# Second bias seeded into the down accumulators, SiLU read from PSUM, and a chunk's last down products done tile by tile

## The chip, the core and the metric

The kernel runs on one core of a Trainium2 chip. Its time is the device time of one execution in microseconds (us). It is written in a tile language: the program names its tiles and pools, buffers of a pool rotate under a tag, and each engine executes its own instructions strictly in the order in which they stand in the program. The engines are TensorE (PE in the profile; its weight loads are PEld), VectorE (DVE), ScalarE (ACT), GpSimd (POOL) and SyncE (SP), which here only issues transfers. Transfers are issued from SP and from ScalarE.

## What is computed

A gated block over x of 2048 tokens and 512 channels: an attention over a short dilated window, multiplied by the SiLU of an MLP, added to x. Everything is float32.

```python
xn = layernorm(x)                                   # over 512 channels, no affine part
# attention: 32 heads of 16, each token sees itself and 7 earlier ones, 2 apart
qkv = xn @ wqkv                                     # 512 -> 3 * 512
s = softmax(q . k[pos - 2*w] / 4, w = 0..7) . v     # positions before 0 are masked
s = s @ wo                                          # 512 -> 512
# MLP: 512 -> 1792 -> 512, squared ReLU
h = maximum(xn @ w1 + b1, 0) ** 2
g = silu(h @ w2 + b2)
out = x + s * g
```

## The kernel before

**Precision.** A product that needs float32 accuracy is done as three products of a faster 32-bit form. Each operand is split into a high part (ScalarE rounds it, `high`) and a low part (the difference, `low`, on VectorE or GpSimd), and TensorE forms high x high, high x low and low x high (`PASSES`). A tile with a leading axis of 2 holds the two parts. A product of 512 columns is the unit in which TensorE works.

**First stage, the projections.** 16 token tiles of 128 are taken in pairs (`for a in range(2, NT, 2)`). `norm` normalises a tile, `shuffle` writes it through four transfers into `xb`, `trans` transposes it on VectorE into PSUM, and `highx` and `lowx` split it into `xt`. From pair 4 on, `pair_of_seven` forms q and k of the two tiles from seven half-size products instead of eight: sums of parts of x (`Sf`, split into `S`) meet sums of weights (`T1` to `T4`), whose parts are made by `split_sum`. Three accumulators (`pm`) and one or two more (`pq`) share four PSUM buffers of the tag `acc`. `u2` keeps one part product until the last sum, which VectorE forms into `stg`. `plan` says behind which of six steps of a pair each piece of work for the next pair is issued; `n` shifts the preparation of the next pair by whole steps. q, k and v go through memory (`sq`, `sk`, `sv`), since the attention wants another layout. Normalised and transposed x of tiles 4 to 15 goes to memory too (`sx`), to be read again by the MLP.

**The attention** is a generator (`attention`). For each unit of 256 tokens VectorE does four multiplications with the keys (`pr`) and four reductions (`L`), the softmax with ScalarE and GpSimd, then four multiplications with the values (`pv`) and four reductions (`v`). `pump` is called between the products and issues as much of this VectorE work as the program's own clock of TensorE allows, so that VectorE's order is fixed when the program is built. Loads of k, q and v are issued from ScalarE; results go to memory (`so`) and come back as `oq` (`load_o`) for the output projection (`trans_o`, `lowo`, `out_product`, into `pw`).

**Second stage, the MLP**, in four chunks of 512 tokens (`for c in range(NCH)`), each of four tiles `j`. `up(c, f)` multiplies the chunk's transposed x (`xT[c]`) with 128 of the 1792 hidden columns, 12 products; ScalarE then applies bias and ReLU in place in PSUM, squares into the high part of `h`, and squares once more, into `hf` or in place; GpSimd or VectorE subtracts to get the low part. `down(pb, f, j)` adds three products for tile j into its accumulator `pb[j]`; the four of them use the four `acc` buffers. `down` follows `up` by two values of f. At a chunk's end stand the downs of f = 12 and 13, f by f. Then `gate` copies each accumulator with ScalarE to `z`, GpSimd adds the second bias `b2t`, and after the next chunk's first two ups `silu` applies SiLU in place. In the last chunk VectorE adds the bias. `finish` multiplies `z` by the output projection, adds x and stores. x of the next chunk is loaded by `load_xT` behind `up(c, 13)`, in two transfers, into the one buffer that the chunk leaves.

Of the kernel before, what the change touches and what calls it, by code (L numbers as in the profile page):

```python
# [57 lines left out]
def body(ctx: ExitStack, tc: tile.TileContext, x, wqkv, wo, w1, b1, w2, b2, out):  # L58
# [141 lines left out]
            G.memset(mask[:GR, :(W - 1 - w) * DIL, w], -1e9)  # L200

    b1t = const.tile([P, NF], F32, name="b1t")

    sq = dram.tile([GR, S, CH], F32, name="sq")
# [195 lines left out]


    NT = S // P
    mv, means, rs, shifts, xn, xb, pTs, xt, xT, seen, Sf, Sp = ({} for _ in range(12))

    def moments(t, st):
        mv[t] = px.tile([P, 2], F32, name=f"mv{t}", tag="mv", bufs=2)
# [40 lines left out]

    def place(t):  # L450
        if t < TPC:
            xt[t] = xT[0][:, t]
        else:
            xt[t] = pxT.tile([P, 2, KT, P], FR, name=f"xt{t}", tag="xt", bufs=4)

    def shuffle(t):

# [37 lines left out]
    def copy_quarter(a):  # L495

        _, pb = quarters(a)
        Sf[a] = hpool.tile([P, 4, 2 * P], F32, name=f"Sf{a}", tag="h", bufs=3)
        A.activation(Sf[a][:, 3], pb[:, 0], AF.Copy)
        seen[a, "copy"] = clock["V"] + 1600  # L500

# [12 lines left out]
    def sum_parts(a, half):  # L514
        n = 2 * half
        flat = Sf[a][:, n:n + 2].rearrange("p j m -> p (j m)")
        if (a, half) not in Sp:
            Sp[a, half] = hpool.tile([P, 2, 2, 2, P], FR, name=f"S{a}_{half}", tag="h", bufs=3)
        return (*(Sp[a, half][:, i].rearrange("p j k n -> p (j k n)") for i in range(2)), flat)

    def high_sums(a, half):
# [53 lines left out]
        done[1][t // 2] = clock["PE"]  # L575

    def load_xT(c):
        xT[c] = xTa.tile([P, TPC, 2, KT, P], FR, name=f"xU{c}", tag="xT")
        for j in range(0, TPC, 2):
            A.dma_start(xT[c][:, j:j + 2].bitcast(F32), sx[c][:, j:j + 2])  # L580

    hs = {}

    def up(c, f):
        ph = psH(f"ph{c}_{f}")
        n = 0
        for kt in range(KT):
            for a, b in PASSES:
                PE.matmul(ph.rearrange("p (j n) -> p j n", n=P), w12[f][:, a, 0, kt * P:(kt + 1) * P],
                          xT[c][:, :, b, kt, :], start=n == 0, stop=n == 11)  # L590
                n += 1
        if f == NF - 1 and c + 1 < NCH:
            load_xT(c + 1)
        h = hpool.tile([P, 2, 512], FR, name=f"h{c}_{f}", tag="h", bufs=3)
        A.activation(ph, ph, AF.Relu, bias=b1t[:, f:f + 1])
        A.activation(h[:, 0], ph, AF.Square)

        pool = c or f < 2 or f > 11
        full = hpool.tile([P, 512], F32, name=f"hf{c}_{f}", tag="hf") if pool else ph
        A.activation(full, ph, AF.Square)  # L600
        if pool:
            G.tensor_sub(h[:, 1], full, h[:, 0].bitcast(F32))
        hs[f] = h, None if pool else ph, clock["PE"] + 2000
# [16 lines left out]
    stats(0)  # L620
    high(*wq_parts(1, 0))
    norm(0)
    xT[0] = xTa.tile([P, TPC, 2, KT, P], FR, name="xT0", tag="xT")
    place(0)
    pT = [psT(f"pxT0_{kt}") for kt in (0, 2)]
    for kt in range(KT):
# [1 line left out]
    stats(1)  # L628
    low(*wq_parts(1, 0), V)

    x0 = hpool.tile([P, D], F32, name="xT0f", tag="h", bufs=3)
# [58 lines left out]
    flush(clock["PE"])  # L690

    split_sum(T1, V)
    split_sum(T4, V)
    pump(LATE)


# [59 lines left out]
    def pair_of_seven(a):  # L756

        b, last = a + 1, a + 2 == NT
        new_stg(a, 1)
        new_stg(a, 0)  # L760
        q, k = stgs[0], stgs[1]
        sums_ps, first, five = (psA(f"pm{a}_{n}") for n in range(3))
        u2 = pstg.tile([P, GR, CH], F32, name=f"u2_{a}", tag="u2")
# [12 lines left out]

        def seventh():
            product(sums_ps, part_s(a, 2), T3, False)
            A.activation(q[:, :, 1], heads(sums_ps), AF.Copy)
            G.tensor_add(k[:, :, 1], k[:, :, 1], q[:, :, 1])  # L780
            product(five, part_s(a, 3), K1, False)
            not_before(clock["PE"])
            V.tensor_add(k[:, :, 0], u2, heads(five))
            store_qkv(b, 1)
            beside(a, 3)

        if last:
            for f in range(2):
                up(0, f)
                pump()  # L790
            lowh(0)
        qkv(b, 2, seventh)
        beside(a, 4)
        product(sums_ps, part_x(b, 1), T4, False)
        A.activation(q[:, :, 1], heads(sums_ps), AF.Copy)
        store_qkv(b, 0)
        beside(a, 5)

    for a in range(2, NT, 2):
        if a >= TPC:  # L800
            for t in (a, a + 1):
                queue(sx[t // TPC][:, t % TPC], xt[t].bitcast(F32))
        (pair_of_seven if a in SEVEN else pair)(a)
        if a == NT - 4:
            dma(b1t, b1.rearrange("(f p) -> p f", p=P))
    pump()
    lowh(1)
    p1ctx.close()


    p2 = ctx.enter_context(tc.tile_pool(name="p2", bufs=1))
    pws, gs = {}, {}
# [57 lines left out]

    xrs = {}

# [10 lines left out]
        dma(tile_rows(out, t)[:, cols], z[:, cols])  # L883

    wot = p2.tile([P, 2, 4, 512], FR, name="wot")
    b2t = p2.tile([P, D], F32, name="b2t")
    rwo = {}

    for c in range(NCH):
        last = c == NCH - 1  # L890
        pb = [psA(f"pb{c}_{j}") for j in range(TPC)]
        t0 = c * TPC
        room = ROOM if c else ROOM0
        for f in range(2, NF):
# [1 line left out]
            if c == 0:  # L896
                next_w()
            pump()
            if c == 0 and f == 8:
                dma(b2t, b2[None, :].to_broadcast([P, D]))  # L900
            if c == 0 and f in (3, 6):

                i = f // 6
# [34 lines left out]
            if f == 11:  # L938
                for i in range(2):
                    lowo(t0 + i)  # L940
            if f >= 12:
                load_o(c * 2 + 1, last and f > 12)
# [67 lines left out]
```

## Time and profile before

| | |
|---|---|
| median of 3 runs | 493.02 us (491.42 to 495.7) |
| profiled execution | 491.57 us |
| its span, first to last instruction | 489.7 us |
| granted TensorE clock, mean | 0.996 |
| busy share: TensorE, VectorE, ScalarE, GpSimd | 98%, 87%, 48%, 47% |
| bytes moved | 81.47 MB |

In profile rows of groups, the form is: line, engine, operation, output from inputs by the program's names, shapes, count, busy time and mean of one, and idle time before with what ended it. Almost all work stands at line 87, the helper that records every operation in program order, so names of tiles tell more than lines. In timeline rows the first two numbers are start and length, and several like instructions are merged with their count; the pipelined products overlap, so a row's length is a little more than its count times their distance. ACTq and SPq rows are issues of transfers. Rows of windows give, per stretch, its length, busy time and count of PE, PEld, DVE, ACT and POOL, the granted clock as a share of full speed, the share of the transfer engines, and GB/s.

### The profile page before, as it was taken

The page shows a single profiled execution, that of the slowest core. Times are in us where ns is not written, and L with a number is a line of the kernel's source. Part 1 is how long each engine was busy: PE and PEld are TensorE (multiplying, and loading weights), DVE is VectorE, ACT ScalarE, POOL GpSimd, SP SyncE. Part 2 cuts the span into 40 slices and gives each one's busy share as a digit, 9 for nine tenths or more (in the row PEclk, how much of TensorE's full clock was granted, in tenths as well). Part 3 has the DMA queues.
Part 4 walks back from the last instruction along what each step waited for, and adds up shares of the span by engine and source line. Part 5 has one row for each costly group of instructions (what it writes and reads, how often), then busy time and mean ns, then how long its engine had stood idle before and what let it go on. Part 6 is the DMA issues. An engine that isn't in the chain of part 4 may idle for free.

```text
span 489.7 us, 5949 instructions
## 1 busy us (share of the span) xinstructions
PE 481.4 (98%) x2118; PEld 395.1 (81%) x2118; DVE 426.5 (87%) x356; ACT 233.0 (48%) x417; POOL 232.3 (47%) x174
## 2 busy tenths in 40 slices
PE   8999999999999999998999999999999999999997
PEld 5888688888888888886888888888888888888886
DVE  5978858987789699996999999699999999999744
ACT  5557597646545655234432333554233364423331
POOL 1325142133665678266847353765534396355310
PEclk9999999999999999998999999999999999999999
DMA  8899999899768984762526356525452763313132
GB/s 289 216 271 271 305 274 259 194 277 299 212 173 201 270 197 129 219 153 37 157 54 165 86 128 211 125 86 124 124 128 56 241 146 107 82 35 93 44 129 88
DMA packets 65530, 81.47 MB, mean 166 GB/s; under 512 B 6108, under 2 KB 49372, under 8 KB 64732
## 3 DMA queue, kind: packets, MB, share of 16 engines
q1 hardware_dynamic: 61180, 54.87, 40.0%
q10 hardware_dynamic: 4320, 26.22, 21.6%
q8 instruction: 17, 0.28, 0.2%
q14 instruction: 13, 0.11, 0.1%
HBM read 50.60 MB, written 27.32 MB: 159 GB/s over the span
## 4 chain that ended last, share of the span: by engine, by line
PE 89%; DVE 4%; issue 3%; POOL 1%; ACT 1%; DMA 1%; ACTq 0%; POOLq 0%; DVEq 0%
PE pb L87 28%; PE ph L87 28%; PE pq L87 13%; PE pm L87 11%; PE pw L87 8%; DVE v L87 1%; DVE pv L87 1%; POOL h L87 1%; POOL z L87 1%; DMA x<-in_A_x 1%; DVE L L87 0%; PE pxT L87 0%; ACT z L87 0%; ACT ph L87 0%; ACT w L87 0%
## 5 line engine op out<-in xcount | busy, mean ns | idle before, releaser
L87 PE MATMUL pb<-w,h 128*128 128x512 f32 x672 | 162.5, 392 | 1.9 <-POOL h L87 1.9
L87 PEld LDWEIGHTS pb<-w,h 128*128 128x128 f32 x672 | 127.1, 189 | 28.8 <-POOL h L87 2.3
L87 POOL TENSOR_TENSOR h<-hf,h 128x512 fp32r<-128x512 f32 x46 | 78.7, 1712 | 101.5 <-ACT hf L87 92.9
L87 PE MATMUL ph<-xU,w 128*128 128x512 f32 x504 | 120.6, 389 | 0.0
L87 PEld LDWEIGHTS ph<-xU,w 128*128 128x128 f32 x504 | 94.7, 188 | 19.7
L87 ACT ACTIVATE ph<-ph,b1t 128x512 f32<-128x512 f32 x56 | 37.0, 662 | 140.4 <-PE ph L87 128.9
L87 DVE TENSOR_TENSOR pr<-k,q 128x2048 f32<-128x2048 f32 x32 | 82.1, 2566 | 3.9 <-DMA q<-sq 3.4
L87 DVE TENSOR_TENSOR pv<-v,L 128x2048 f32<-128x2048 f32 x32 | 77.4, 2419 | 2.0 <-POOL L L87 1.2
L87 DVE TENSOR_REDUCE v<-pv 128x256 f32<-128x2048 f32 x32 | 73.0, 2281 | 0.8
L87 DVE TENSOR_REDUCE L<-pr 128x128 f32<-128x2048 f32 x32 | 73.0, 2281 | 0.7
L87 PE MATMUL pw<-wot,oT 128*128 128x512 f32 (+1 forms) x204 | 45.9, 376 | 0.0
L87 PEld LDWEIGHTS pw<-wot,oT 128*128 128x128 f32 x204 | 36.8, 188 | 7.1
L87 PE MATMUL ph<-xT,w 128*128 128x512 f32 x168 | 40.2, 389 | 0.0
L87 POOL TENSOR_TENSOR w<-w1r,w 128x512 fp32r<-128x512 f32 x14 | 22.5, 1608 | 33.0 <-ACT w L87 33.0
L87 PEld LDWEIGHTS ph<-xT,w 128*128 128x128 f32 x168 | 31.5, 188 | 6.5
L87 PE MATMUL pm<-wq,S 128*128 128x512 f32 x144 | 36.2, 392 | 0.2 <-ACT S L87 0.2
L87 PE MATMUL pq<-wq,xt 128*128 128x512 f32 x144 | 35.8, 390 | 0.0
L87 ACT ACTIVATE h<-ph 128x512 fp32r<-128x512 f32 x56 | 33.5, 599 | 1.8
L87 ACT ACTIVATE hf<-ph 128x512 f32<-128x512 f32 x46 | 27.4, 595 | 11.4 <-POOL h L87 11.4
L87 PEld LDWEIGHTS pm<-wq,S 128*128 128x128 f32 x144 | 26.7, 188 | 7.1 <-ACT S L87 0.7
L87 PEld LDWEIGHTS pq<-wq,xt 128*128 128x128 f32 x144 | 26.9, 188 | 6.2 <-ACT stg L87 0.6
L87 PE MATMUL pq<-wq,xT 128*128 128x512 f32 x132 | 30.9, 393 | 0.0
(83 smaller groups left out, 507.6 us busy)
## 6 DMA issues: line engine op xcount, KB each, us to landing
k<-sk ACTq DMA_DIRECT2D x8, 960.0 KB, 7.4
v<-sv ACTq DMA_DIRECT2D x8, 960.0 KB, 8.4
sx<-xt SPq DMA_DIRECT2D x12, 512.0 KB, 5.5
xU<-sx ACTq DMA_DIRECT2D x6, 1024.0 KB, 7.4
x<-in_A_x SPq DMA_DIRECT2D x16, 256.0 KB, 4.9
sk<-stg SPq DMA_DIRECT2D x8, 512.0 KB, 4.0
sq<-stg SPq DMA_DIRECT2D x8, 512.0 KB, 6.5
sv<-stg SPq DMA_DIRECT2D x8, 512.0 KB, 4.9
```

Of the source, the lines that this page charges most:

```text
L87: return tc.keep_in_program_order(f(*a, **k))
```

## The change

The second bias is loaded early, beside `b1t`, and kept. Before a chunk's downs ScalarE copies it into each accumulator (`begin`), and all downs add to it (`start=False`). At a chunk's end the downs of f = 10 are held back behind `up(c, 13)`; the downs of f = 12 and 13 are done tile by tile, and behind each tile ScalarE applies SiLU from PSUM to `z` (`gate`) and seeds the accumulator for the next chunk. The separate bias additions and `silu` are gone.

The transposed x keeps the channel block `kt` as its outer axis: `sx` is written in pieces of 1 KB instead of 4 KB, and `load_xT` loads a chunk in four transfers, one for each `kt`. In the projections, pair 4 prepares the next pair one step earlier (`n` is 1 instead of 2 there); two of the weight differences and the split of T4 move from VectorE to GpSimd and into pair 2; `Sf`, `S` and `h` have four buffers instead of three; `u2` moves into the buffers of `hf` and `x`. `load_o` of a chunk's second unit is issued at other places.

```diff
-    sx = {c: dram.tile([P, TPC, 2, KT, P], F32, name=f"sx{c}") for c in range(1, NCH)}
+    sx = {c: dram.tile([P, KT, TPC, 2, P], F32, name=f"sx{c}") for c in range(1, NCH)}
...
     def load_xT(c):
-        xT[c] = xTa.tile([P, TPC, 2, KT, P], FR, name=f"xU{c}", tag="xT")
-        for j in range(0, TPC, 2):
-            A.dma_start(xT[c][:, j:j + 2].bitcast(F32), sx[c][:, j:j + 2])
+        xT[c] = xTa.tile([P, KT, TPC, 2, P], FR, name=f"xU{c}", tag="xT")
+        for kt in range(KT):
+            A.dma_start(xT[c][:, kt].bitcast(F32), sx[c][:, kt])
...
-        h = hpool.tile([P, 2, 512], FR, name=f"h{c}_{f}", tag="h", bufs=3)
+        h = hpool.tile([P, 2, 512], FR, name=f"h{c}_{f}", tag="h", bufs=4)
...
-            V.tensor_sub(*(raws[s, kt + i] for s, kt in (d, x0, x1)))
+            (G if d == (0, 2) else V).tensor_sub(*(raws[s, kt + i] for s, kt in (d, x0, x1)))
...
     split_sum(T1, V)
-    split_sum(T4, V)
     pump(LATE)
...
-        n, t = (2 if a < 6 else 0), a + 2
+        n, t = {2: 2, 4: 1}.get(a, 0), a + 2
...
-    for i, w in enumerate((T2, T3)):
+    for i, w in enumerate((T2, T3, T4)):
         at(2, 1 + i, split_sum, w, G)
...
-                queue(sx[t // TPC][:, t % TPC], xt[t].bitcast(F32))
+                queue(sx[t // TPC][:, :, t % TPC], xts[t].bitcast(F32))
...
+    def begin(c, j):
+
+        pbs[c, j] = psA(f"pb{c}_{j}")
+        A.activation(pbs[c, j], b2t, AF.Copy)
+
     def down(pb, f, j):
         h, w = hs[f][0], w12[f]
         for n, (a, b) in enumerate(PASSES):
             PE.matmul(pb[j], h[:, a, j * P:(j + 1) * P], w[:, b, 1, :],
-                      start=f == 0 and n == 0, stop=f == NF - 1 and n == 2)
+                      start=False, stop=f == NF - 1 and n == 2, skip_group_check=True)
...
     def gate(c, j, pb):
         z = gs[c, j] = piece(f"z{c}_{j}")
-        if c == NCH - 1:
-            V.tensor_add(z, pb[j], b2t)
-            silu(c, j)
-        else:
-            A.activation(z, pb[j], AF.Copy)
-            G.tensor_add(z, z, b2t)
-
-    def silu(c, j):
-        A.activation(gs[c, j], gs[c, j], AF.Silu)
+        A.activation(z, pb[j], AF.Silu)
...
-            if not (last and f == NF - 1):
+            downs = [f - 2]
+            if last and f == NF - 1:
+                downs = []
+            elif not last and f > NF - 3:
+                downs = [f - 3, f - 2] if f == NF - 1 else []
+            for i in downs:
                 for j in range(TPC):
-                    down(pb, f - 2, j)
+                    down(pb, i, j)
...
         if not last:
-            for i in range(2):
-                for j in range(TPC):
+            for j in range(TPC):
+                for i in range(2):
                     down(pb, NF - 2 + i, j)
-                if i == 0:
-                    pump(room)
-            pump()
-            for j in range(TPC):
+                pump(room if j < 2 else -SLACK)
                 gate(c, j, pb)
+                begin(c + 1, j)
             for i in range(2):
                 up(c + 1, i)
                 pump(ROOM)
                 lowh(i)
-            for j in range(TPC):
-                silu(c, j)
+                load_o(c * 2 + 1, False)
             out_product(t0 + 1, psT(f"pw{t0 + 1}"))
             pump(ROOM)
```

More of the change, by code (lines that the diff above doesn't have):

```diff
@@ L202, in body @@
     b1t = const.tile([P, NF], F32, name="b1t")
+    b2t = const.tile([P, D], F32, name="b2t")
     sq = dram.tile([GR, S, CH], F32, name="sq")
@@ L404, in body @@
     NT = S // P
-    mv, means, rs, shifts, xn, xb, pTs, xt, xT, seen, Sf, Sp = ({} for _ in range(12))
+    mv, means, rs, shifts, xn, xb, pTs, xt, xT, seen, Sf, Sp, xts = ({} for _ in range(13))
     def moments(t, st):
@@ L451, in place @@
         if t < TPC:
-            xt[t] = xT[0][:, t]
+            parts = xT[0][:, :, t]
         else:
-            xt[t] = pxT.tile([P, 2, KT, P], FR, name=f"xt{t}", tag="xt", bufs=4)
+            parts = xts[t] = pxT.tile([P, KT, 2, P], FR, name=f"xt{t}", tag="xt", bufs=4)
+        xt[t] = parts.rearrange("p k a n -> p a k n")
     def shuffle(t):
@@ L497, in copy_quarter @@
         _, pb = quarters(a)
-        Sf[a] = hpool.tile([P, 4, 2 * P], F32, name=f"Sf{a}", tag="h", bufs=3)
+        Sf[a] = hpool.tile([P, 4, 2 * P], F32, name=f"Sf{a}", tag="h", bufs=4)
         A.activation(Sf[a][:, 3], pb[:, 0], AF.Copy)
@@ L517, in sum_parts @@
         if (a, half) not in Sp:
-            Sp[a, half] = hpool.tile([P, 2, 2, 2, P], FR, name=f"S{a}_{half}", tag="h", bufs=3)
+            Sp[a, half] = hpool.tile([P, 2, 2, 2, P], FR, name=f"S{a}_{half}", tag="h", bufs=4)
         return (*(Sp[a, half][:, i].rearrange("p j k n -> p (j k n)") for i in range(2)), flat)
@@ L622, in body @@
     norm(0)
-    xT[0] = xTa.tile([P, TPC, 2, KT, P], FR, name="xT0", tag="xT")
+    xT[0] = xTa.tile([P, KT, TPC, 2, P], FR, name="xT0", tag="xT")
     place(0)
@@ L629, in body @@
     low(*wq_parts(1, 0), V)
-    x0 = hpool.tile([P, D], F32, name="xT0f", tag="h", bufs=3)
+    x0 = hpool.tile([P, D], F32, name="xT0f", tag="h", bufs=4)
     for kt in (0, 2):
@@ L762, in pair_of_seven @@
         sums_ps, first, five = (psA(f"pm{a}_{n}") for n in range(3))
-        u2 = pstg.tile([P, GR, CH], F32, name=f"u2_{a}", tag="u2")
+        home = dict(pool=px, tag="x", bufs=4) if last else dict(pool=hpool, tag="hf")
+        u2 = home.pop("pool").tile([P, GR, CH], F32, name=f"u2_{a}", **home)
         product(sums_ps, part_x(a, 0), Q0)
@@ L805, in body @@
             dma(b1t, b1.rearrange("(f p) -> p f", p=P))
+            dma(b2t, b2[None, :].to_broadcast([P, D]))
     pump()
@@ L885, in body @@
     wot = p2.tile([P, 2, 4, 512], FR, name="wot")
-    b2t = p2.tile([P, D], F32, name="b2t")
     rwo = {}
@@ L890, in body @@
         last = c == NCH - 1
-        pb = [psA(f"pb{c}_{j}") for j in range(TPC)]
+        if c == 0:
+            for j in range(TPC):
+                begin(c, j)
+        pb = [pbs[c, j] for j in range(TPC)]
         t0 = c * TPC
@@ L940, in body @@
                     lowo(t0 + i)
-            if f >= 12:
-                load_o(c * 2 + 1, last and f > 12)
-            if not (last and f == NF - 1):
+            if f == 11 or (last and f > 11):
+                load_o(c * 2 + 1, f > 12)
+            downs = [f - 2]
[4 more added lines that the diff above has]
+            for i in downs:
                 for j in range(TPC):
-                    down(pb, f - 2, j)
+                    down(pb, i, j)
             pump(room)
@@ L952, in body @@
         if not last:
-            for i in range(2):
-                for j in range(TPC):
+            for j in range(TPC):
+                for i in range(2):
                     down(pb, NF - 2 + i, j)
-                if i == 0:
-                    pump(room)
-            pump()
-            for j in range(TPC):
+                pump(room if j < 2 else -SLACK)
                 gate(c, j, pb)
+                begin(c + 1, j)
             for i in range(2):
```

6 lines of the change are left out of this document (2 added, 4 removed).

## The prediction

> **What bounds the kernel now.** I read the page's busy table first, then the chain of waits that ended last, and then the TensorE timeline wherever that chain leaves TensorE.
>
> ```profile
> span 489.7 us, 5949 instructions
> PE 481.4 (98%) x2118; PEld 395.1 (81%) x2118; DVE 426.5 (87%) x356; ACT 233.0 (48%) x417; POOL 232.3 (47%) x174
> ...
> 303.66 5.44 PE ph L87 x24
> ```
>
> TensorE is busy for 98% of the span, and the chain shows its pace: 24 products of 512 columns in 5.44 us, 0.2267 us each. The change neither adds nor removes a product, so it can win only where products start later than this pace allows. I walked the TensorE timeline of the whole span and compared each group's start with the previous start plus count times 0.2267. Behind the opening 11 us, two places miss by more than 0.15 us. The first is in the projections:
>
> ```profile
> 55.38 1.98 PE L87 MATMUL pm<-wq,xt 128*128 128x512 f32 x8
> 57.82 1.20 PE L87 MATMUL pm<-wq,xt 128*128 128x512 f32 x4 [0.47 <-DVE xt L87]
> 59.27 1.92 PE L87 MATMUL pm<-wq,S 128*128 128x512 f32 x6 [0.25 <-ACT S L87]
> 61.21 3.02 PE L87 MATMUL pq<-wq,xt 128*128 128x512 f32 x12
> ```
>
> From 55.38, 8 + 4 + 6 products should take 4.08 us and end at 59.46; the next group starts at 61.21. That is 1.75 us lost, for xt, for S, and for a free accumulator. The second place is the start of MLP chunk 1:
>
> ```profile
> 223.55 0.61 PE L87 MATMUL pb<-w,h 128*128 128x512 f32 x2
> 226.04 4.14 PE L87 MATMUL pb<-w,h 128*128 128x512 f32 x10 [1.87 <-POOL h L87]
> 230.02 2.24 PE L87 MATMUL ph<-xU,w 128*128 128x512 f32 x9
> ...
> 224.00:226.00 2.00, 0.17 (x1) 0.00 (x0) 0.86 (x1) 0.00 (x0) 1.98 (x1) 1.00 0.00 0
> 226.00:228.00 2.00, 1.96 (x6) 1.52 (x7) 0.00 (x0) 1.95 (x3) 1.27 (x1) 0.63 0.04 8
> 228.00:229.00 1.00, 1.00 (x4) 0.81 (x3) 0.41 (x1) 1.00 (x3) 0.00 (x0) 0.50 0.00 0
> 229.00:230.00 1.00, 1.00 (x4) 0.79 (x3) 1.00 (x2) 1.00 (x3) 0.00 (x0) 0.54 0.00 0
> ```
>
> Two products from 223.55 end at 224.00 and the third starts at 226.04: 2.04 us of waiting for GpSimd's low part of h. The next ten should take 2.27 us and take 3.98: another 1.71. The windows (the column behind the five engines is the granted clock) show why: 0.63, 0.50 and 0.54 between 226 and 230; behind it nine products take 2.24 us, full pace again. The wait costs 3.75 us, nearly half of it as lost clock. Everything that can be won is thus 3.75 + 1.75 = 5.5 us, 1.1%.
>
> The Trainium skill, "TensorE: Matmul & The Clock Gate", Part 1, has the clock halve after an idle window of about 3.4 us. Here 2.04 us were enough, so the rows decide; by the page's figure alone this stall would be priced at 2.04 us and the forecast would be 1.71 us later.
>
> **What makes h late at 226.** GpSimd and ScalarE around the chunk's end:
>
> ```profile
> 214.30 0.53 ACTq L87 DMA_DIRECT2D v<-sv  x1
> 214.88 2.06 ACT L87 ACTIVATE z<-pb 128x512 f32<-128x512 f32 x4 [10.23 <-issue]
> 216.80 0.70 ACT L87 ACTIVATE ph<-ph,b1t 128x512 f32<-128x512 f32 x1
> ...
> 218.03 0.60 ACT L87 ACTIVATE hf<-ph 128x512 f32<-128x512 f32 x1
> ...
> 215.61 7.11 POOL L87 TENSOR_TENSOR z<-z,b2t 128x512 f32<-128x512 f32 x4 [0.85 <-POOL L L87]
> 222.67 3.31 POOL L87 TENSOR_TENSOR h<-hf,h 128x512 fp32r<-128x512 f32 x1
> ```
>
> ScalarE stands at the v load until 214.30, then copies four accumulators; GpSimd adds the second bias to them for 7.11 us, and only then splits h, until 225.98.
>
> **The second bias, SiLU, tile by tile: -3.75 us.** The change removes those four additions (12 in all; at the later two chunk starts TensorE does not wait). In the built program ScalarE now takes, per token tile, one SiLU from PSUM and one Copy that seeds the next accumulator. The v load stands behind the third pair, ahead of the fourth. If the load is released at 214.30 as before, the fourth pair ends about 1.65 us later (0.53 of issue, two activations of about 0.55), at 215.95; relu and two squares take 218.63 - 216.80 = 1.83, to 217.8; GpSimd's subtraction then takes between 1.36 (half of a two-piece row shown further down) and 3.31: h is whole at 219.2 to 221.1. It is needed by the third product, 223.55 + 0.45 = 224.0. Slack is 2.9 to 4.8 us, less some 0.9 by which TensorE now arrives earlier. So both the wait and its clock loss go. Bounds: 0 (it stays) to 3.75.
>
> Beside it: a SiLU and a seed need about 1.05 us per tile, at the 0.52 us pitch of the four z<-pb activations, while TensorE gives a tile's last six products in 1.36, so ScalarE keeps up. The table for SiLU is loaded between the last h of the chunk and the first tile, where ScalarE idled 10.23 us (214.88 row), and is not loaded back. Four seeds before chunk 0 (2.1 us) lie beside the 12 products (2.72 us) of up 2; without that cover they cost 0.52 each. Holding back the downs of h10 only reorders products; h13's split gains cover, since 5.44 + 2.72 us of products stand ahead of its use. At the end of the kernel the four bias additions on VectorE lie under the last products and the span's last multiply, addition and store are untouched: 0.
>
> **The x reload: 0.** Its issues, its time to landing, and the queues:
>
> ```profile
> 201.99 0.83 ACTq L87 DMA_DIRECT2D xU<-sx  x2
> ...
> xU<-sx ACTq DMA_DIRECT2D x6, 1024.0 KB, 7.4
> ...
> q1 hardware_dynamic: 61180, 54.87, 40.0%
> q10 hardware_dynamic: 4320, 26.22, 21.6%
> ```
>
> Four issues instead of two keep ScalarE 1.7 us instead of 0.83. The load may start when up 13 ends, and now 24 + 12 + 24 products (13.6 us) instead of 48 (10.9) lie between that and its first use, against 7.4 us to landing: covered. The stores now write 512 pieces of 1 KB where they wrote 128 of 4 KB. The queue table bounds the cost: a packet of q1 (0.90 KB) takes 0.400 x 16 x 489.7 / 61180 = 51 ns, one of q10 (6.1 KB) 392 ns. Time goes by bytes, so I take 0. Were those 51 ns all fixed cost, a store would take 384 x 0.051 / 16 = 1.2 us longer. The early broadcast of the second bias (256 KB) stands behind all early weight loads: at q10's 15.5 bytes per ns on 16 engines it is 1.1 us of transfer, in front of a store that TensorE does not wait for: 0.
>
> **Pair 4 a step earlier, T4 on GpSimd: -1.15 + 0.3.** VectorE in that stretch, and what ScalarE does between S and the accumulator's copy:
>
> ```profile
> 47.77 2.29 DVE L87 TENSOR_REDUCE L<-pr 128x128 f32<-128x2048 f32 x1
> 49.97 1.31 DVE L87 STREAM_TRANSPOSE pxT<-xb 128x512 f32<-128x512 f32 x2
> 51.19 2.27 DVE L87 TENSOR_TENSOR pr<-k,q 128x2048 f32<-128x2048 f32 x1
> 54.29 0.69 DVE L87 TENSOR_TENSOR stg<-u,pm 128x512 f32<-128x512 f32 x1 [0.83 <-PE pm L87]
> 54.89 2.28 DVE L87 TENSOR_REDUCE L<-pr 128x128 f32<-128x2048 f32 x1
> 57.09 0.68 DVE L87 TENSOR_TENSOR xt<-pxT,xt 128x512 fp32r<-128x512 f32 x1
> ...
> 58.47 0.88 DVE L87 TENSOR_TENSOR Sf<-pxT,Sf 128x256 f32<-128x256 f32 x2
> ...
> 58.59 0.63 ACT L87 ACTIVATE S<-Sf 128x512 fp32r<-128x512 f32 x1 [2.41 <-DVE Sf L87]
> ...
> 60.58 0.58 ACT L87 ACTIVATE stg<-pm 128x512 f32<-128x512 f32 x1
> ...
> L100 SPq DMA_DIRECT2D xb<-xn x4: 593/598/2393, 40.3 to 44.0; - x4
> ...
> DMA to landing us min/median/max: 4.1/4.3/4.3
> ```
>
> In the built order the transposes precede the first reduction, and the second reduction moves behind xt and the S lows. The transposes wait for the last xb piece, issued at 44.0 and landed 4.3 us later, at 48.3; transposes, reduction and multiplication (1.3 + 2.3 + 2.3 us) then end at 54.2, just in time for stg at 54.29. So xt comes 2.2 us sooner, at 54.9 instead of 57.09, ahead of the 57.19 at which TensorE stopped for it, and S by the same amount. What stays is the accumulator: the copy at 60.58 starts 1.99 us behind the S activation before it, since ScalarE's statistics lie between. Now the second S high stands there first: its sums end at 59.35 - 2.2 = 57.15, it starts near 57.45, the copy near 59.45, its end near 60.05 against 59.46 for TensorE. So 0.6 of 1.75 stays, and 1.15 goes (bounds 0.4 to 1.75).
>
> T4's two differences and two splits leave VectorE and run on GpSimd behind T3's:
>
> ```profile
> 38.67 2.71 POOL L87 TENSOR_TENSOR wq<-wqraw,wq 128x512 fp32r<-128x512 f32 x2
> ...
> 38.74 1.50 DVE L87 TENSOR_SCALAR xn<-x,mv,rs 128x512 f32<-128x512 f32 x1 [0.45 <-POOL rs L87]
> ...
> 42.33 0.68 DVE L87 TENSOR_TENSOR S<-Sf,S 128x512 fp32r<-128x512 f32 x1
> ...
> 43.06 1.52 PE L87 MATMUL pm<-wq,S 128*128 128x512 f32 x6
> ```
>
> They would fill GpSimd from 41.4 to 44.1, where VectorE makes S. A VectorE row beside GpSimd work grew to 1.50 us, some 0.8 beyond an S row. S at 42.33 may thus come up to 0.9 us late. It ends at 43.01, and the third product of its group needs it at 43.06 + 0.45, so 0.5 us is slack: cost 0 to 0.4, and up to 0.9 if xt behind it is caught too; I take 0.3.
>
> The Trainium skill, "SBUF — State Buffer", section "Who interferes with whom", says that a VectorE instruction with two SBUF inputs and a GpSimd instruction that reads SBUF block each other for a whole instruction. By it S would wait up to one GpSimd subtraction, 1.36 us, and 0.9 instead of 0.3 would be lost there.
>
> **Sum.** -3.75 - 1.15 + 0.3 = -4.6. The profiled execution took 491.57 us (span 489.7 and 1.9 around it): 491.57 - 4.6 = 487.0. The median of the three runs shown is 493.02, 1.45 above the profiled one, and one run is 4.1 above, so a median of the changed kernel may lie above its profile too.
>
> **Rivals.**
> - *The boundary wait stays.* If the v load is released 3 us later, or GpSimd's normalisation of L slips, h is late again. For it: one ScalarE queue carries the load, SiLU and relu. Against it: about 2 us of slack and no bias additions. Time: 491.57 - 0.85 = 490.7.
> - *The early step does nothing.* If xb lands some 2 us later than at 48.3, VectorE waits, and xt is as late as now. For it: VectorE then has 0.1 us to spare at stg. Against it: the four pieces all landed within 4.1 to 4.3 us. Time: 491.57 - 3.75 + 0.3 = 488.1.
> - *Slower: 1 KB pieces delay xb.* The two sx stores of a pair stand ahead of the next xb pieces on one queue. If each takes its bound of 1.2 us more, xb lands 2.4 us later. This decides once it exceeds what VectorE waits for TensorE in a pair:
>
> ```profile
> DVE stg L87 <- PE pm L87: 10.6, 4, 5.4
> ```
>
>   In four of six pairs VectorE has 2.65 us on average; two have none. With three pairs stalling 2.4 us, each followed by 1.71 us of lost clock, it costs 12.4 us, less the gains: 491.57 + 12.4 - 4.6 = 499.4, or 494.3 with the clock kept; I put it at 497. Against it: time goes by bytes in the queue table.
>
> **How the numbers follow.** Forecast 0.62 (its own range 485.6 to 488.8); early step nothing 0.14 (488.1); boundary wait stays 0.13 (490.7); slower 0.11 (497). The range 485.4 to 492.0 starts where both stalls vanish (491.57 - 5.5 = 486.1, less the run-to-run difference), and takes in the two weaker cases. About 1% is what a measurement of this kernel can tell from no change: 493.02 less 1% is 488.1, 491.57 less 1% is 486.7. So the forecast lies on the edge: seven tenths of it and a third of the second case count as faster, 0.48; slower is 0.10; the rest, 0.42, is within 1%.
>
> **What would show it.** Right: no TensorE idle and granted clock 1.00 where chunk 1 starts; no POOL z<-z,b2t row; the gap of that projection group shrinks to about 0.6; same 0.2267 pace elsewhere. Wrong: a PE wait on ACT or POOL near the first downs of a chunk, a clock below 1.00 behind it, DVE waits on DMA xb, or more than 2 us lost around 43 or 57 us.

## The result and the profile after

| | before | after |
|---|---|---|
| median | 495.06 us (491.42 to 497.13, 6 runs) | 488.43 us (487.27 to 489.83, 6 runs) |
| profiled execution | 491.57 us | 488.73 us |
| its span | 489.7 us | 486.8 us |

The changed kernel takes 0.9875 of the time before, 95% interval 0.9835 to 0.9916. The forecast was 487.0. The profiled execution became 2.8 us shorter where 4.6 had been forecast; the medians moved by 6.6. Both differences need an explanation, and so does the narrower spread (the spans of the changed kernel's six runs lie within 485.5 and 488.0 us). Ratios, here and below, leave out single runs that lie more than 1.5% above the fastest of their kernel.

The head of the page of the changed kernel:

```profile
span 486.8 us, 5931 instructions
PE 478.8 (98%) x2118; PEld 393.8 (81%) x2118; DVE 417.6 (86%) x348; ACT 235.1 (48%) x421; POOL 204.1 (42%) x166
```

GpSimd (POOL) lost 28 us of work, and TensorE's count of products is the same. The start of MLP chunk 1, in the TensorE timeline and the windows around it:

```profile
221.56 2.88 PE L87 MATMUL ph<-xU,w 128*128 128x512 f32 x12
224.28 2.88 PE L87 MATMUL pb<-w,h 128*128 128x512 f32 x12
227.00 2.88 PE L87 MATMUL ph<-xU,w 128*128 128x512 f32 x12
...
216.00:222.00 6.00, 6.00 (x28) 4.97 (x27) 5.90 (x4) 4.04 (x8) 2.80 (x2) 1.00 1.02 209
222.00:228.00 6.00, 6.00 (x28) 4.97 (x27) 5.97 (x4) 1.75 (x3) 1.85 (x3) 1.00 0.24 39
```

Twelve downs (pb) now run in one piece, 2.72 us from start to start, where two of them were followed by 2.04 us of nothing; the granted clock (third number from the right) is 1.00. What feeds them, on ScalarE and GpSimd:

```profile
200.00 2.61 ACTq L87 DMA_DIRECT2D xU<-sx  x4
...
204.45 1.28 ACT L87 ACT_TABLE_LOAD   x1
209.52 0.60 ACT L87 ACTIVATE z<-pb 128x512 f32<-128x512 f32 x1 [3.79 <-PE pb L87]
...
214.83 0.54 ACTq L87 DMA_DIRECT2D v<-sv  x1
215.42 0.60 ACT L87 ACTIVATE z<-pb 128x512 f32<-128x512 f32 x1 [1.94 <-DMA so<-v]
...
218.43 1.70 POOL L87 TENSOR_TENSOR h<-hf,h 128x512 fp32r<-128x512 f32 x1 [3.16 <-ACT hf L87]
220.90 1.29 POOL L87 TENSOR_TENSOR h<-hf,h 128x512 fp32r<-128x512 f32 x1 [0.78 <-ACT hf L87]
```

The low part of h is whole at 218.43 + 1.70 = 220.13; the third down needs it at 224.28 + 0.45 = 224.73. The old wait has become 4.6 us of slack, although the v load, still waiting for the store of the attention's results (so<-v), is issued at 214.83, half a microsecond later than before.

The projection group near 60 us, on TensorE, VectorE and ScalarE:

```profile
55.52 2.88 PE L87 MATMUL pm<-wq,xt 128*128 128x512 f32 x12
58.24 1.52 PE L87 MATMUL pm<-wq,S 128*128 128x512 f32 x6
60.36 1.90 PE L87 MATMUL pq<-wq,xt 128*128 128x512 f32 x7 [0.60 <-ACT stg L87]
...
48.91 1.32 DVE L87 STREAM_TRANSPOSE pxT<-xb 128x512 f32<-128x512 f32 x2 [1.02 <-DMA xb<-xn]
55.23 0.68 DVE L87 TENSOR_TENSOR xt<-pxT,xt 128x512 fp32r<-128x512 f32 x1
...
59.73 0.58 ACT L87 ACTIVATE stg<-pm 128x512 f32<-128x512 f32 x1
```

The waits for xt and S are gone; six S products from 58.24 end at 59.60, and 0.76 us pass until ScalarE's copy has freed the accumulator. So far the forecast. Then a place that it had not named, first in the changed kernel, then in the kernel before:

```profile
109.63 1.52 PE L87 MATMUL pm<-wq,xt 128*128 128x512 f32 x6
112.22 1.66 PE L87 MATMUL pq<-wq,xt 128*128 128x512 f32 x6 [1.07 <-ACT stg L87]
113.97 2.35 PE L87 MATMUL pm<-wq,S 128*128 128x512 f32 x9
...
111.57 0.60 ACT L87 ACTIVATE stg<-pq 128x512 f32<-128x512 f32 x1 [5.22 <-DMA sk<-stg]
```

```profile
102.94 0.38 SPq L100 DMA_DIRECT2D sk<-stg  x1
...
DMA to landing us min/median/max: 7.8/7.8/7.8
...
110.42 1.52 PE L87 MATMUL pm<-wq,xt 128*128 128x512 f32 x6
111.78 1.52 PE L87 MATMUL pq<-wq,xt 128*128 128x512 f32 x6
113.25 0.97 PE L87 MATMUL pm<-wq,S 128*128 128x512 f32 x3
...
110.86 0.60 ACT L87 ACTIVATE stg<-pq 128x512 f32<-128x512 f32 x1 [3.72 <-DMA sk<-stg]
```

TensorE reaches this pair 0.79 us sooner (109.63 against 110.42) and leaves it 0.72 later (113.97 against 113.25). The accumulator that it wants next is copied by ScalarE into a staging buffer (stg), and that buffer is still being stored as k (sk<-stg). ScalarE waited there before too, 3.72 us, but its copy was done at 110.86 + 0.60 = 111.46, ahead of the need at 111.78; only the next copy, behind it, held TensorE up by 0.11 us, at 113.25. The store itself moved with TensorE: it is issued at 102.17 in the changed kernel, 0.77 sooner than before (the row is shown with the later weights below). But it takes 9.3 us to land instead of 7.8.

The start of the same group in both kernels gives the whole account:

| group | after minus before | change |
|---|---|---|
| pm<-wq,xt near 55 us | +0.14 us | |
| pq<-wq,xt near 60 us | -0.85 us | -0.99, the first stage |
| pm<-wq,xt near 110 us | -0.79 us | +0.06 |
| pm<-wq,S near 113 us | +0.72 us | +1.51, the k store |
| first downs of chunk 1 | +0.73 us | +0.01 |
| the ups behind them | -3.02 us | -3.75, chunk 1's start |
| span | -2.9 us | +0.1 |

### The profile page after: what moved, and what is told of

The parts are those of the page before. It is cut to its first block, busy times and chain, and to the rows that moved or that the text cites. A ratio compares the mean times of both kernels' runs of the same rounds, so it can differ in the third digit from the quotient of the medians.

```text
span 486.8 us, 5931 instructions
## 1 busy us (share of the span) xinstructions
PE 478.8 (98%) x2118; PEld 393.8 (81%) x2118; DVE 417.6 (86%) x348; ACT 235.1 (48%) x421; POOL 204.1 (42%) x166
## 4 chain that ended last, share of the span: by engine, by line
PE 87%; DMA 5%; DVE 4%; ACT 2%; issue 1%; SPq 0%; POOL 0%; DVEq 0%; ACTq 0%; POOLq 0%
PE pb L87 31%; PE ph L87 31%; PE pq L87 10%; PE pw L87 9%; PE pm L87 5%; DMA sk<-stg 2%; DMA sx<-xt 1%; DVE L L87 1%; DMA xb<-xn 1%; DMA x<-in_A_x 1%; DVE pxT L87 1%; SPq L100 0%; ACT stg L87 0%; DVE pr L87 0%; ACT mean L87 0%
## 5 line engine op out<-in xcount | busy, mean ns | idle before, releaser
L87 PE MATMUL pb<-w,h 128*128 128x512 f32 x672 | 160.1, 389 | 0.0
L87 POOL TENSOR_TENSOR h<-hf,h 128x512 fp32r<-128x512 f32 x46 | 72.5, 1576 | 152.0 <-ACT hf L87 152.0
L87 DVE TENSOR_TENSOR pr<-k,q 128x2048 f32<-128x2048 f32 x32 | 78.9, 2466 | 4.4 <-DMA q<-sq 3.9
L87 DVE TENSOR_TENSOR pv<-v,L 128x2048 f32<-128x2048 f32 x32 | 75.4, 2355 | 6.3 <-POOL L L87 5.5
L87 PEld LDWEIGHTS pq<-wq,xT 128*128 128x128 f32 x132 | 24.5, 188 | 5.8 <-ACT xT L87 0.7
(82 smaller groups left out, 486.8 us busy)
```

What stands on the lines that cost most here:

```text
L87: return tc.keep_in_program_order(f(*a, **k))
```

## The experiments

Each ratio is against the kernel before, measured on the same chip beside it.

**The additions of the second bias alone.** In the kernel before:

```diff
             A.activation(z, pb[j], AF.Copy)
-            G.tensor_add(z, z, b2t)
```

> The kernel before with the twelve GpSimd additions of the second bias left out in chunks 0 to 2 (the output lacks that bias there); order of products, gates and SiLU as before. Theory (GpSimd's queue is what makes h late at chunk 1): the 2.04 us wait at 226 and the 1.71 us of lost clock go, profiled span 486.0 +- 0.4, and the runs lie 1.0 to 1.4% below the kernel before, since chunk 2's start, with 0.3 us to spare before, is relieved too. Rival (ScalarE, held by the v load until 214.3, or the order of the downs is the cause): the wait stays, span 489 to 490, ratio 0.997 to 1.003.

489.56 us (489.28 to 489.99, 4 runs), ratio 0.9886 (0.9853 to 0.9919); span 487.5. TensorE does not wait at chunk 1, and the spans of the four runs lie within 487.5 and 488.1. One line reproduces nearly the whole result, its narrow spread with it. The profiled span misses the expected 486.0 because of the k store, although this kernel's projections are those of the kernel before:

```profile
110.61 1.52 PE L87 MATMUL pm<-wq,xt 128*128 128x512 f32 x6
113.07 1.65 PE L87 MATMUL pq<-wq,xt 128*128 128x512 f32 x6 [0.94 <-ACT stg L87]
```

Here 1.10 us are lost at 113.07 and 0.38 behind it, with a landing of 9.2 us. So this loss does not need the change's first stage.

**The MLP part alone**: seeds, SiLU from PSUM and the new order of the downs; projections and x as before.

```diff
+        A.activation(pbs[c, j], b2t, AF.Copy)
...
-                      start=f == 0 and n == 0, stop=f == NF - 1 and n == 2)
+                      start=False, stop=f == NF - 1 and n == 2, skip_group_check=True)
...
-            G.tensor_add(z, z, b2t)
...
+        A.activation(z, pb[j], AF.Silu)
```

> The change's MLP part alone: seeds, SiLU from PSUM, downs tile by tile, downs of h10 held back; projections and x layout as before. Theory: same gain as leaving the additions out, span 486.0 +- 0.5, ratio 0.986 to 0.990, and no wait at 112 us. Rival (the first stage carries a good part): span 488 or more, ratio above 0.993.

490.04 us (489.55 to 490.33), ratio 0.9894 (0.986 to 0.9927); span 488.0, clock 1.00, no wait at chunk 1. The expected span of 486.0 and the absence of a wait at 112 us missed: the k store took 9.4 us to land, and 1.70 us are lost there, again with the old projections. The ratio is the expected one. It is not faster than the removal alone: the new order brings nothing beside it that these runs can show, and seeding is a way to drop the additions and keep the bias.

**The first stage alone** (with the buffers that it needs):

```diff
-            V.tensor_sub(*(raws[s, kt + i] for s, kt in (d, x0, x1)))
+            (G if d == (0, 2) else V).tensor_sub(*(raws[s, kt + i] for s, kt in (d, x0, x1)))
...
-    split_sum(T4, V)
...
-        n, t = (2 if a < 6 else 0), a + 2
+        n, t = {2: 2, 4: 1}.get(a, 0), a + 2
...
-    for i, w in enumerate((T2, T3)):
+    for i, w in enumerate((T2, T3, T4)):
```

> The change's first stage alone: pair 4 a step earlier, T4 on GpSimd, four buffers, u2 elsewhere. Theory: about 1.0 us won at 57 to 61, some of it lost at 112 because TensorE arrives sooner at the same store; the wait at chunk 1 stays: span 488.8 to 489.7, ratio 0.997 to 1.001. Rival: it carries much of the gain, ratio below 0.994.

494.16 us (490.97 to 498.49, 10 runs), ratio 0.9957 (0.9921 to 0.9994). In its profile 0.57 us are left of the stall near 60 us instead of 1.75; chunk 1 still starts with a wait of 2.37 us and 1.64 of lost clock. The k store is issued at 101.94 and lands in 8.1 us, and only 0.35 us are lost there. The spans scatter, from 489.2 to 493.9 in nine of the ten runs, as those of the kernel before do.

**The layout of x alone, and the changed kernel with the old layout**:

```diff
-        xT[c] = xTa.tile([P, TPC, 2, KT, P], FR, name=f"xU{c}", tag="xT")
-        for j in range(0, TPC, 2):
-            A.dma_start(xT[c][:, j:j + 2].bitcast(F32), sx[c][:, j:j + 2])
+        xT[c] = xTa.tile([P, KT, TPC, 2, P], FR, name=f"xU{c}", tag="xT")
+        for kt in range(KT):
+            A.dma_start(xT[c][:, kt].bitcast(F32), sx[c][:, kt])
```

> The x layout alone: sx written in 1 KB pieces, x reloaded in four transfers. Theory A (time goes by bytes): nothing, span 489.4 to 490.0, ratio 0.998 to 1.002, no new wait at 112. Theory B (the pieces delay the store of k, which delays the copy at 112): 0.4 to 1.4 us later at 112, the k store lands 9 us or more behind its issue, span 490 to 491, ratio 1.001 to 1.004.

> The changed kernel with the old x layout (4 KB pieces, two transfers). If the pieces delay the k store: the 1.23 us gap at 112 shrinks to 0.4 or less, span 485.5 to 486.0. If TensorE merely arrives sooner at an equally late store: the gap stays at 0.4 to 1.2 and the span at 486.3 to 486.9.

The first: 495.05 us (10 runs), ratio 0.9995 (0.9967 to 1.0023). The second, with everything but this: 488.88 us (488.19 to 489.62), ratio 0.9866 (0.9799 to 0.9933). The layout is worth nothing that these runs can show. The second also clears the 1 KB pieces of the wait at 112 us: without them it is there, 1.49 and 0.38 us of lost start in its profile, more than either theory had expected, with a landing of 9.6 us. The first has it too, 1.56 us with a landing of 9.3, and its span of 492.6 lies above what both of its theories gave.

**The kernel before, once more**, without an edit, for its spread.

> The kernel before once more, for the span and the granted clock of each of its runs. Theory: its runs differ because a chunk start sometimes waits more (span up by 1 to 6 us, mean clock down by 0.004 to 0.010 with it). Rival: spans agree and only the time around the span varies, or the clock is the same in all.

496.35 us (491.9 to 498.11, 10 runs), ratio 1.0028 (0.9987 to 1.007). Its spans reach from 490.1 to 496.3 us with a mean clock of 0.995 to 0.997 in every run. So the scatter belongs to the kernel before, and it is not in the clock, where the expectation had put part of it: at the same clock, the longer runs must wait longer somewhere.

**Three additions instead of four** in each chunk, and **eight operations instead of four** (for two tiles of each chunk the bias is added, taken away and added again):

```diff
+            if j < 3:
+                G.tensor_add(z, z, b2t)
```

```diff
+            if j > 1:
+                G.tensor_sub(z, z, b2t)
+                G.tensor_add(z, z, b2t)
```

> The kernel before with three instead of four GpSimd additions at each chunk's end (tile 3 lacks the second bias). GpSimd then reaches h 1.3 to 1.8 us sooner: the wait at chunk 1 falls from 2.04 to 0.3 to 0.8 us. If lost clock follows any wait in proportion: 0.2 to 0.7 us of it. If it needs a long enough idle time: none, granted clock 1.00 throughout, span 486.2 to 487.0.

> The kernel before with four more GpSimd operations at each chunk's end (the bias is subtracted and added again for tiles 2 and 3, same result). Each costs 1.3 to 1.8 us, so h comes 5.2 to 7.1 us later: at every chunk start TensorE waits 5 to 9 us instead of 2.04, 0 and 0. Lost clock in proportion to the wait: 4 to 7 us behind each. Lost clock of a fixed stretch: 1.5 to 2 us behind each, as in the kernel before. Span 506 to 515 by the second.

Three: 490.47 us, span 488.7, one execution. The wait at chunk 1 is gone altogether (three additions end at 222.46, h at 223.70, just ahead of the need at 224.2), but one has come up a chunk later, and the span is above the expected 486.2 to 487.0. GpSimd, TensorE and the windows there:

```profile
306.59 5.81 POOL L87 TENSOR_TENSOR z<-z,b2t 128x512 f32<-128x512 f32 x3
312.36 1.26 POOL L87 TENSOR_TENSOR h<-hf,h 128x512 fp32r<-128x512 f32 x1
...
310.80 0.61 PE L87 MATMUL pb<-w,h 128*128 128x512 f32 x2
313.68 2.58 PE L87 MATMUL pb<-w,h 128*128 128x512 f32 x10 [2.27 <-POOL h L87]
...
312.00:314.00 2.00, 0.32 (x1) 0.30 (x2) 1.59 (x1) 0.34 (x1) 1.63 (x2) 1.00 0.98 205
314.00:316.00 2.00, 2.00 (x10) 1.63 (x9) 0.00 (x0) 1.97 (x3) 1.29 (x1) 1.00 0.96 165
```

Even three additions are late when the work ahead of them is late, and what was expected of the place was wrong. Eight: 509.48 us, span 507.7, mean clock 0.982, and a wait at each of the three chunk starts, 7.34, 4.48 and 3.26 us, of which only the first lies within the expected 5 to 9. The lost clock behind them, 2.53, 1.66 and 1.73 us, is near the fixed stretch of 1.5 to 2 and far from a proportion. The first:

```profile
216.33 14.46 POOL L87 TENSOR_TENSOR z<-z,b2t 128x512 f32<-128x512 f32 x8 [0.85 <-POOL L L87]
...
224.27 0.61 PE L87 MATMUL pb<-w,h 128*128 128x512 f32 x2
232.06 4.64 PE L87 MATMUL pb<-w,h 128*128 128x512 f32 x10 [7.18 <-POOL h L87]
...
228.00:234.00 6.00, 1.94 (x5) 1.57 (x6) 0.00 (x0) 1.93 (x3) 5.13 (x5) 0.50 0.01 3
```

GpSimd's 14.46 us instead of 7.11 lengthen the wait from 2.04 to 7.34. That is one for one: 7.35 us more of additions, less the 2.05 by which the low part of h behind them is shorter here (1.26 us instead of 3.31), is 5.30, as is 7.34 - 2.04.

**The additions left out in the first chunk only**:

```diff
-            G.tensor_add(z, z, b2t)
+            if c: G.tensor_add(z, z, b2t)
```

> The kernel before, with the four additions of the second bias left out in the first chunk only (its four output tiles lack that bias); the eight additions of the next two chunks stay. Theory: what the other executions of the kernel before lose beyond the profiled one (spans of 490 to 498 us against 487 to 488 without any of the additions) is lost at the start of the second chunk alone, where the chain from the v store to h is exposed: then the profile shows no wait at the start of the second chunk, the spans lie at 487 to 489 us and the ratio at 0.988 to 0.990. Rival: the additions of the two later chunks cost in those executions too, since GpSimd is only some 0.3 us ahead of the need at the start of the third chunk: then spans reach 490 to 495 us, and the ratio is 0.992 to 0.996.

489.22 us (488.49 to 491.72, 4 runs), ratio 0.9886 (0.9814 to 0.9958); spans 486.6, 487.4, 487.5 and 489.9. The ratio is that of leaving out all twelve, though its interval reaches into the rival's range. TensorE does not stop at chunk 1:

```profile
225.02 2.88 PE L87 MATMUL pb<-w,h 128*128 128x512 f32 x12
```

**Two later steps in the changed kernel, each alone and both together.** The first moves two ScalarE statistics of token tile 10 behind the accumulator's copy, the second moves a weight split with its two loads from the third to the last step of pair 10, behind the k store:

```diff
-             10: ((4, 4), (4, 5), (6, 0), (6, 1)), 12: ((6, 2), (6, 3), (6, 4), (6, 5)),
+             10: ((4, 5), (4, 5), (6, 0), (6, 1)), 12: ((6, 2), (6, 3), (6, 4), (6, 5)),
```

```diff
-    ahead = {(10, 2): 1, (12, 4): 1, (14, 0): 1, (14, 2): 1, (14, 4): 1}
+    ahead = {(10, 5): 1, (12, 4): 1, (14, 0): 1, (14, 2): 1, (14, 4): 1}
```

> The changed kernel with one step moved: ScalarE's statistics of token tile 10 (two activations) are issued a step later, behind the copy of the pair's accumulator instead of ahead of it. Theory (the rest of the projection stall near 60 us is ScalarE's order): the 0.76 us without products there goes to under 0.3, the span falls from 486.8 by 0.4 to 0.8, and the median by as much, about 487.8 against 488.4. Rival (the accumulator's release is bound by VectorE's sums before the second S): the gap stays at 0.6 to 0.8, and nothing changes.

> The changed kernel with the first split of the MLP weights, and the two loads of 256 KB that it sends, moved from the third to the last step of pair 10. Theory (the wait at 112 us is the k store's landing behind those two loads, which stand right ahead of it on SyncE's queue): the store of k that TensorE's accumulator waits for through ScalarE lands 1.5 to 3 us sooner, the 1.6 us without products at 112 to 114 go, and the span falls by about 1.5, to 485.3. Rival (the store is late by itself, whatever stands ahead of it): the gap stays in those executions that show it, and the span stays at 486 to 488.

> The changed kernel with both moves: statistics of tile 10 a step later, first weight split and its loads at the last step of pair 10. If both theories hold the gains add: span about 484.8, median some 2 us below the changed kernel, ratio to the kernel before about 0.983. If only one holds, 485.3 to 486.3; if neither, 486.8.

Statistics later: 488.78 us (487.63 to 489.72), ratio 0.9867 (0.9799 to 0.9936); span 487.9. TensorE and ScalarE in its profile:

```profile
43.24 0.73 PE L87 MATMUL pm<-wq,S 128*128 128x512 f32 x2
44.16 1.20 PE L87 MATMUL pm<-wq,S 128*128 128x512 f32 x4 [0.18 <-DVE S L87]
...
58.91 1.52 PE L87 MATMUL pm<-wq,S 128*128 128x512 f32 x6
60.27 1.98 PE L87 MATMUL pq<-wq,xt 128*128 128x512 f32 x8
...
65.80 1.66 PE L87 MATMUL pq<-wq,xt 128*128 128x512 f32 x6
68.23 2.11 PE L87 MATMUL pm<-wq,S 128*128 128x512 f32 x8 [0.78 <-ACT u L87]
...
65.15 0.60 ACT L87 ACTIVATE stg<-pq 128x512 f32<-128x512 f32 x1 [1.08 <-DMA sk<-stg]
67.56 0.62 ACT L87 ACTIVATE u<-pm 128x512 f32<-128x512 f32 x1
```

The order on ScalarE was the reason for the 0.76 us: they are gone, 58.91 + 6 x 0.2267 = 60.27. TensorE comes to this place 0.67 us later here, which by itself would hide most of them, but with both steps moved it comes at 58.05 and loses nothing either. But the kernel is no faster, because the time is lost again six microseconds later: 1.07 us behind 65.80, for an accumulator that ScalarE copies (u) behind a staging copy that waits for another k store. (The wait at 112 us is there as well, 1.71 us.) In the changed kernel itself that copy also waits, 0.59 us, and TensorE arrives just late enough not to notice.

Weights later: 488.46 us (487.38 to 489.12), ratio 0.9866 (0.9786 to 0.9946), span 485.6. The issues on SyncE's queue and the landing of this one k store (its minimum, median and maximum are one value), in the changed kernel and then with the weights later:

```profile
100.92 0.35 SPq L391 DMA_DIRECT2D w2r<-in_B_w  x1
102.17 0.37 SPq L100 DMA_DIRECT2D sk<-stg  x1
...
DMA to landing us min/median/max: 9.3/9.3/9.3
```

```profile
101.63 0.37 SPq L100 DMA_DIRECT2D sk<-stg  x1
107.41 1.44 SPq L390 DMA_DIRECT2D w1r<-in_B_w  x1
...
DMA to landing us min/median/max: 7.1/7.1/7.1
```

The store lands in 7.1 us instead of 9.3, and the wait at 112 us is gone from this profile and from the next. Its median, however, lies only 0.3 us below that with the statistics later. In the profiles of the other kernels, all with the loads ahead of the store, the wait comes and goes with the landing:

| profile | store to landing | lost near 112 us |
|---|---|---|
| weights later; both later | 7.1; 7.2 us | 0 |
| before; before again; three additions; eight operations | 7.8 each | 0.1 each |
| first stage alone | 8.1 | 0.35 |
| no additions; none in the first chunk | 9.2 each | 1.48; 1.49 |
| x layout alone; changed kernel | 9.3 each | 1.56; 1.62 |
| MLP part alone; statistics later | 9.4 each | 1.70; 1.71 |
| changed kernel with the old x layout | 9.6 | 1.87 |

Up to this store the kernel before and the two kernels of the fourth row are the same program, since their edits come in at a chunk's end. So no edit makes the difference between 7.8 and 9.2 us.

Both: 486.71 us (486.24 to 486.96, 4 runs), ratio 0.9825 (0.9759 to 0.9892), span 484.9. This is the fastest of all; every run of it is below every run of the other two on the same chip, and its spans agree within 0.7 us. The sum of the two theories had given a span of 484.8 and a ratio of 0.983, but not by the parts that the theories named: the wait for u near 67 us is there too, 0.82 us. Why the pair's median is 1.75 us better than that of the later weights alone is not settled. Their profiles lie 0.7 us apart: the later weights alone lose 1.10 us near 61 and 0.37 near 45, and the pair loses 0.82 near 67 instead.

## Why the prediction was right, and where it was not

*Chunk 1's start, -3.75: right, to the hundredth in the profiled execution.* Wait and lost clock both went. The steps held: a tile's SiLU and seed follow TensorE's 1.36 us per tile (the first three z<-pb stand at 209.52, 210.88 and 212.24), the table load of 1.28 us lies in ScalarE's idle time, and h was forecast whole at 219.2 to 221.1 and was at 220.13. Of GpSimd's subtraction the forecast left 1.36 to 3.31 open; it takes 1.70 and 1.29.

*First stage, -1.15: measured -0.99, and -1.18 by itself.* The forecast had xb at 48.3 (transposes waited until 48.91), xt at 54.9 (55.23), the accumulator's copy at 59.45 (59.73), and 0.6 left of the stall (0.76). VectorE did wait 1.02 us for xb, but not long enough to matter: the rival that the early step does nothing fell.

*T4 on GpSimd, +0.3 with bounds of 0 and 0.9: 0 in the profiled execution.* S took 0.87 us instead of 0.68 at that place, and the six S products start 1.36 apart from their neighbours. (The 1.50 us row from which the forecast took its 0.9 is another operation.) The bound was not idle, though: with the statistics later 0.66 us were lost there (0.19 and 0.47 around 43.24 and 44.16), when the normalisation ahead of it came 0.7 us later. By the Trainium skill, "SBUF — State Buffer", section "Who interferes with whom", a VectorE instruction with two SBUF inputs and a GpSimd instruction that reads SBUF contend for an exclusive lock. The trace agrees. S started at 42.55, while a GpSimd subtraction ran from 41.56 to 42.86, and ended 0.19 us late; the subtraction behind that one took 1.75 us instead of 1.30. S met only the end of a subtraction, so the whole one that the forecast named as the most did not come up.

Where chunk 1 starts in the kernel before, the same meeting cost much more. VectorE's multiplication of k and q stood beside the last addition and the low part of h:

```profile
221.41 3.45 DVE L87 TENSOR_TENSOR pr<-k,q 128x2048 f32<-128x2048 f32 x1
```

It took 3.45 us instead of 2.29, and the low part of h, which GpSimd started at 222.67, took 3.31 instead of 1.29. One of the four additions took 3.36 us, the other three 1.29 each. With eight operations the low part of h came when VectorE had nothing to do, and took 1.26; without the additions it came earlier, beside a reduction, and took 1.29. So two of GpSimd's instructions ahead of TensorE's need took 2.0 us longer each beside VectorE's multiplications, and the additions had put them there. The forecast took the 7.11 and the 3.31 from the rows and did not ask what they were made of.

*x reload, 0: right.* ScalarE spent 2.61 us on the four issues instead of the 1.7 estimated, and nothing waited for it. A store of x landed in 5.7 us instead of 5.5, so the slower rival, which needed 1.2 us per store, had nothing to stand on. (Its price adds up to 12.3, three times 2.4 + 1.71, rather than 12.4.)

*What the sum lacked: a term for the k store near 112 us.* At 110.86 of the old profile the row with 3.72 us of waiting for sk<-stg said that ScalarE was bound by a store there, 0.3 us ahead of TensorE's need, and the next copy behind it already cost 0.11 us; the forecast asked only where TensorE lost more than 0.15. The store landed in 7.8 us in the profiled execution of the kernel before and in 9.3 in that of the changed kernel, and 1.51 us more were lost. It is not the first stage's gain that was taken back, since the store moved with TensorE: the first stage alone lost 0.35 us there with a landing of 8.1, and four kernels with the old projections lost 1.48 to 1.70 with landings of 9.2 to 9.4. Nor was it the change's transfers, since the old layout shows it as well. What makes the landing 7.8 or over 9 us with the loads ahead of it stays open. From -4.6 this leads to -3.1; the first stage's 0.16 less, the 0.3 for T4 that was not lost, and 0.31 of small shifts (the first line of the account, and its two of 0.06 and 0.01, and the end) lead to the -2.9. With like landings the profiled difference would have been about -4.35 (an estimate: -2.84 - 1.51), close to the -4.6.

*The median: the step from the profiled execution to the median was wrong.* The forecast expected the changed kernel's median above its profile, as before. It lay 0.3 below. That 488.43 came out near 487.0 is thus partly luck: the forecast started from an execution of the kernel before that was 3.5 us shorter than its median (491.57 against 495.06), and the change took that excess away. The spread of the kernel before belongs in the main to the additions: spans of 489.2 to 497.6 us in the kernels that have them all, 484.5 to 488.5 in the seven without any, and 486.6 to 489.9 with the first chunk's additions alone left out. There they stand between the v load, which waits for VectorE's store, and h, so lateness of VectorE reaches TensorE at once; without them 4.6 us of slack take it up. That most of the longer executions are longer at this place is inferred from what removing it does. One profile, that of the x layout alone, is of a longer execution, with a span of 492.6 us. Against the 489.7 of the kernel before it loses 1.45 us more at the k store and 1.02 more at the start of chunk 1 (3.00 + 1.77 against 2.04 + 1.71), where the v load is issued at 216.71 instead of 214.30. No profile of a kernel with the four additions has a span of 494 us or more, and what grows in such executions stays open.

## What to carry over

A step that stands between two engines' deadlines costs more than one profile shows: look at the spread of the times, and at what removing the step does to it. Before a difference between two profiles is put down to the change, look for it in kernels that leave that part of the program alone; here 1.5 us at a store showed up in four kernels with the old projections, and stood for a third of the forecast gain. A row in which an engine waits for a store and is only just in time says where such a difference can enter. And when a stall is removed, walk on along the bottleneck engine: moving two statistics behind a copy removed 0.76 us and uncovered 1.07 six microseconds later. The version with both later steps has the lowest ratio, 0.9825 against 0.9875, but it was not measured beside the changed kernel, and the two intervals overlap.

## What the hardware showed that was not expected

The clock's loss is not in proportion to the idle time. 2.04 us of waiting cost 1.71 us more in the kernel before, and five other waits of 2.10 to 4.48 us cost between 1.64 and 1.77; 7.34 us cost 2.17 us in the ten products behind them and 0.36 later. But 2.43 us in the kernel with three additions cost 0.15, with a granted clock of 1.00 in the windows around it. The Trainium skill, "TensorE: Matmul & The Clock Gate", Part 1, describes a free-running activity window, so that what an idle stretch costs would depend on where in the window it falls. Stretches of like length with unlike results agree with that; its 3.4 us as the needed idle time do not, since 2.04 sufficed.

A k store of 512 KB took 7.1 to 9.6 us to land near 102 us, and 5.3 to 5.8 near 58. The 7.1 and 7.2 are those with the two weight loads issued behind it. With the loads just ahead of it on the same queue it took 7.8 us in four profiles, 8.1 in one and 9.2 to 9.6 in seven, and the same program up to that point gave both 7.8 and 9.2; what decides between them stays open.
